# Decay rows of a four-batch attention kernel: one fp32 sum in place of a high and a low part, no zero rows, stacks made at first use, second job prepared before the first scores

## The chip, the cores and the metric

One core of a Trainium2 chip runs the whole program. The metric is device time in microseconds (us) of one execution, input and output in the chip's memory; a profile of one execution shows what each engine did. The engines are PE (TensorE: matmuls, with PEld its weight loads), DVE (VectorE), ACT (ScalarE), POOL (GpSimd) and SP, which here only issues DMAs, in the order of its program.

## The reference, cut to what matters

Decayed causal attention (4 batches, 8 heads, 576 positions, head size 64) feeds two feed-forward layers (512 to 2048 to 512) over 2304 tokens:

```
scores = (1/sqrt(64)) * q @ k^T
cum    = cumsum(log(clip(f, 1e-4, 1)))           # one number per position
scores = where(causal, scores + cum[i] - cum[j], -1e9)
attn   = softmax(scores);  y = attn @ v
x = y as (2304, 512)
h = x @ w_in;  x = (h * tanh(softplus(h))) @ w_out
h = x @ w2_in; out = (h * cos(h)) @ w2_out
```

## The kernel before

Attention runs as 20 jobs. A job is one pair of heads of one batch; batch 0 is cut into jobs 0 to 3 (query blocks 0 and 1) and jobs 4 to 7 (blocks 2 to 4), batches 1 to 3 have one job for each pair with all five blocks. An item is one block of one job. For an item PE makes the scores (L503 for batch 0, L510 later), DVE adds the mask and takes the row maximum (L553), ACT takes the exponential and its sum (L559), DVE inverts the sum (L570, L571), POOL scales (L573), PE transposes the probabilities three items later (L610, L599), and PE multiplies them by v (L635), from where ACT and DVE write the result `xb` (L647, L648). Once batch 0's first tokens are there, the first layer's matmuls with w_in (L154) are woven between attention items. After attention, only the feed-forward layers are left.

The decay enters the scores as extra rows of the contraction. A stack holds transposed q and transposed k in partitions 0 to 63 (L473 on ACT, L475 on DVE, from PE's transposes L450). In batch 0 (`whole(jb)`, fp32 stacks `stk0`, `stk1`) the rows 64, 65, 96 and 97 hold the decay sum as a high and a low part and the constants -1 and 1 that meet them; the other rows from 64 to 127 are set to zero, and the contraction is 128 rows long. Later jobs use fp32r stacks of four planes (`stkr0`, `stkr1`) in two passes; the second pass carries the decay the same way. Every stack is filled once by four memsets (L656 to L659), each over 32 partitions and 1152 elements.

The decay sum is made by `decay_tables`: a load of f, a clip, Ln, a scan (L751), then the high part on ACT (L753) and the low part on DVE (L754). Job 0's rows are copied from there to the stack by four DMAs (L426); both parts go to a DRAM buffer `cumd` (L434), and every later job's rows come from there (L428). `prep_job(jb)` issues these row copies, then the transposes and casts of q and k, then the loads of job jb+2. The weights of w_in are loaded in pieces of 512 KB (L105, no earlier than the copy to `cumd`) and converted by DVE, POOL and ACT (L124, L125, L129, L134, L138, L139). A scheduler sets the final order of each engine from dependencies and its own costs, so the order on an engine is not the order of the lines.

Of the kernel before, what the change touches and what calls it, by code (L numbers as in the profile page):

```python
# [32 lines left out]
def f(ap):  # L33
    return ap.bitcast(F32)
# [3 lines left out]
def tile_attention_two_ffn(  # L38
# [40 lines left out]
    yd = dram.tile([128, 2, NK, NT], F32, name="yd")  # L79
    cumd = dram.tile([B * H, 2, S], F32, name="cumd")  # L80
# [274 lines left out]
    def attention_units(p, bank):  # L355
# [11 lines left out]
        def whole(jb):  # L367
            return jobs[jb][0] // NP in CUT_BATCHES
# [47 lines left out]
        def prep_job(jb):  # L416
# [6 lines left out]
            for row, x in ((96, 0), (64, 1)) if whole(jb) else ((96, 2), (64, 3)):  # L423
                if jb == 0:
                    for y in range(2):
                        nc.sync.dma_start(out=st[row + y : row + y + 1, x], in_=cums[y][h0 : h0 + 2])  # L426
                else:
                    nc.sync.dma_start(  # L428
                        out=st[row : row + 2, x] if whole(jb) else f(st[row : row + 2, x]),
                        in_=cumd[h0 : h0 + 2].rearrange("h y s -> y h s")  # L430
                    )
            if jb == 0:
                for y in range(2):
                    marks["cum"] = nc.sync.dma_start(out=cumd[:, y], in_=cums[y])  # L434
# [12 lines left out]
            for g in groups:  # L447
# [3 lines left out]
                for which, lo in ((0, qlo), (1, 0)):  # L451
# [14 lines left out]
                    if whole(jb):  # L466
                        for j in range(2):
                            i_ = t[64 * j : 64 * j + 64, at : at + n * P]
                            if jb == 0:
                                i_ = i_.rearrange("r (c p) -> r c p", p=P)  # L470
                            o = part(slice(0, 64), which, j)
                            if which or j:
                                nc.scalar.activation(out=o, in_=i_, func=AF.Copy, scale=sc)  # L473
                            else:
                                nc.vector.tensor_scalar(out=o, in0=i_, scalar1=sc, scalar2=None, op0=ALU.mult)  # L475
                        continue
# [15 lines left out]
        def scores(jb, i):  # L492
# [7 lines left out]
            def product(o, j, c0, c1, first=QS[i], m=r):  # L500
                if whole(jb):
                    at = j * S + first
                    marks["score"] = nc.tensor.matmul(  # L503
                        o, lhsT=st.rearrange("p x j s -> p (x j s)")[0:128, at : at + m],
                        rhs=st[0:128, 1, j, c0:c1], start=True, stop=True,
                    )
                    return
                for x in range(2):
                    at = (4 * x + j) * S + first
                    marks["score"] = nc.tensor.matmul(  # L510
                        o, lhsT=st.rearrange("p x j s -> p (x j s)")[0:128, at : at + m],
                        rhs=st[0:128, 2 * x + 1, j, c0:c1], start=(x == 0), stop=(x == 1),
                    )
# [138 lines left out]
        def new_stack(pool, name, dt, en):  # L652
# [3 lines left out]
            nc.gpsimd.memset(q[96:128], 0.0)  # L656
            nc.gpsimd.memset(k[64:96], 0.0)
            en.memset(q[64:96], -1.0)
            en.memset(k[96:128], 1.0)  # L659
# [19 lines left out]
        stack(late - 1)  # L679
# [4 lines left out]
        for _ in prep_job(0):  # L684
            pass
        prep = None
# [7 lines left out]
        for m in range(2 * (M + LT + 1)):  # L694
# [14 lines left out]
            if m2 < M:  # L709
# [4 lines left out]
                if at == begin:  # L714
                    prep = prep_job(jb + 1)
# [28 lines left out]
    def decay_tables(p):  # L744
# [7 lines left out]
        ch, cl = (x.bitcast(F32R) for x in (ft, one))  # L752
        nc.scalar.activation(out=ch, in_=cum, func=AF.Copy)  # L753
        nc.vector.tensor_tensor(out=cl, in0=cum, in1=ft, op=ALU.subtract)  # L754
        cums.extend((ft, one))
# [140 lines left out]
```

## Time and profile before

| | |
|---|---|
| median of 3 runs | 1055.91 us (1055.45 to 1059.02) |
| the profiled execution | 1053.56 us, span of the trace 1051.8 us |
| PE | busy 1011.2 us, 96% of the span |
| DVE, ACT, POOL | 57%, 51%, 23% |
| DMA | 111.80 MB, mean 106 GB/s |

The profiled execution is itself 2.35 us below the median of the runs. PE is the engine to watch: 40.6 us of the span are not PE, and the question for each of them is which wait ended last.

### The profile page before, as it was taken

What the parts mean: (1) busy time and instruction counts of PE and PEld (TensorE: products, weight loads), DVE (VectorE), ACT (ScalarE), POOL (GpSimd) and SP (SyncE); (2) the same over time, 40 slices, a digit from 0 to 9 for tenths busy, and PEclk for the clock granted to TensorE, in tenths of its full rate; (3) what the DMA queues carried; (4) which work ended last, traced back from release to release, by engine and by line L of the source; (5) the groups of instructions that cost most, each with busy time, mean ns of one, the idle gap of its engine ahead of it and who ended that gap; (6) DMA issues with size and microseconds to landing.
All of it is one profiled execution on the core that took longest, in us unless ns stands there. A gap on an engine that the chain in (4) does not pass through costs nothing.

```text
span 1051.8 us, 16908 instructions
## 1 busy us (share of the span) xinstructions
PE 1011.2 (96%) x5920; PEld 865.8 (82%) x5920; DVE 598.3 (57%) x1402; ACT 537.6 (51%) x1142; POOL 236.9 (23%) x331
## 2 busy tenths in 40 slices
PE   5798899999999999999999999999999999999998
PEld 4586779899999999977778888888888888888897
DVE  5858755666555536746664267766444544454454
ACT  4666746665556536446664465644433333333343
POOL 7647643433323312412120012111000000000000
PEclk9999999999999999999999999999999999999999
DMA  4655423333331138756966365412100300110010
GB/s 118 169 151 123 136 70 95 85 93 89 84 90 60 57 117 277 238 176 196 325 206 223 111 195 177 159 41 71 50 1 1 120 1 1 41 41 1 1 41 21
DMA packets 118361, 111.80 MB, mean 106 GB/s; under 512 B 66564, under 2 KB 87044, under 8 KB 118276
## 3 DMA queue, kind: packets, MB, share of 16 engines
q1 hardware_dynamic: 118276, 110.72, 34.5%
q8 instruction: 47, 0.77, 0.3%
q14 instruction: 38, 0.31, 0.1%
HBM read 77.49 MB, written 33.18 MB: 105 GB/s over the span
## 4 chain that ended last, share of the span: by engine, by line
PE 77%; DMA 8%; DVE 5%; ACT 4%; issue 3%; POOL 3%; SPq 0%; ACTq 0%; POOLq 0%; DVEq 0%
PE h L154 24%; PE acc L257 19%; PE hx L154 9%; DMA hl<-hd 5%; PE s L635 5%; PE acc L249 5%; PE s L610 4%; PE s L510 3%; PE hx L249 2%; PE h L249 2%; PE s L450 2%; PE s L503 2%; DMA raw<-in_moe_w_in_dram 1%; POOL wol L139 1%; DVE gl L319 1%
## 5 line engine op out<-in xcount | busy, mean ns | idle before, releaser
L154 PE MATMUL h<-xb,wih 128*128 128x288 f32 (+2 forms) x848 | 184.2, 305 | 4.0 <-ACT wih L138 2.7
L154 PEld LDWEIGHTS h<-xb,wih 128*128 128x128 f32 x848 | 138.7, 191 | 7.1 <-ACT wih L138 3.2
L154 PE MATMUL h<-xb,wil 128*128 128x288 f32 (+2 forms) x424 | 126.3, 300 | 0.0
L559 ACT ACTIVATE s<-s,mx 128x448 f32<-128x448 f32 (+5 forms) x144 | 83.7, 582 | 68.4 <-DVE mx L553 64.4
L257 PE MATMUL acc<-woh,gh 128*128 128x512 f32 x288 | 112.9, 392 | 0.0
L257 PE MATMUL acc<-woh,gl 128*128 128x512 f32 x288 | 112.3, 391 | 0.0
L257 PE MATMUL acc<-wol,gh 128*128 128x512 f32 x288 | 112.0, 389 | 0.0
L573 POOL TENSOR_SCALAR s<-s,sm 128x448 f32<-128x448 f32 (+5 forms) x144 | 82.8, 588 | 124.4 <-DVE sm L571 63.4
L319 DVE TENSOR_TENSOR gl<-hl,gh 128x512 fp32r<-128x512 f32 x72 | 65.0, 904 | 70.5 <-ACT gh L314 70.4
L154 PE MATMUL hx<-x,wih 128*128 128x512 f32 (+1 forms) x320 | 92.7, 369 | 0.0
L154 PE MATMUL h<-x,wih 128*128 128x512 f32 (+1 forms) x320 | 91.0, 369 | 0.0
L305 ACT ACTIVATE n<-n 128x512 f32<-128x512 f32 (+1 forms) x80 | 47.1, 589 | 85.8 <-DVE n L299 85.6
L139 POOL TENSOR_TENSOR wol<-raw,woh 128x512 fp32r<-128x512 f32 x32 | 45.3, 1416 | 197.6 <-ACT woh L138 174.0
L553 DVE CUSTOM_DVE_ANT_0 s<-s,maskt 128x288 f32<-128x288 f32 (+6 forms) x152 | 63.7, 430 | 45.3 <-PE s L510 24.9
L319 DVE TENSOR_TENSOR gl<-e,gh 128x512 fp32r<-128x512 f32 (+1 forms) x80 | 53.8, 672 | 50.7 <-ACT gh L314 50.5
L154 PEld LDWEIGHTS h<-xb,wil 128*128 128x128 f32 x424 | 79.9, 190 | 1.3 <-issue 0.8
L298 DVE TENSOR_SCALAR n<-e 128x512 f32<-128x512 f32 (+1 forms) x80 | 32.7, 408 | 84.3 <-ACT e L291 83.8
L288 ACT ACTIVATE hl<-hl 128x512 f32<-128x512 f32 x72 | 45.1, 629 | 61.1 <-DMA hl<-hd 59.4
L314 ACT ACTIVATE gh<-e 128x512 fp32r<-128x512 f32 (+1 forms) x80 | 47.1, 588 | 52.3 <-DVE e L310 48.9
L249 PE MATMUL acc<-gl,woh 128*128 128x512 f32 (+1 forms) x192 | 68.5, 358 | 3.3 <-DVE gl L319 3.2
L249 PE MATMUL acc<-gh,wol 128*128 128x512 f32 (+1 forms) x192 | 67.8, 354 | 0.0
L154 PEld LDWEIGHTS h<-x,wih 128*128 128x128 f32 x320 | 58.4, 188 | 11.0
(119 smaller groups left out, 2215.7 us busy)
## 6 DMA issues: line engine op xcount, KB each, us to landing
hl<-hd SPq DMA_DIRECT2D x72, 256.0 KB
raw<-in_moe_w_in_dram SPq DMA_DIRECT2D x32, 512.0 KB
raw<-in_moe_w_out_dram SPq DMA_DIRECT2D x32, 512.0 KB
hd<-hs SPq DMA_DIRECT2D x48, 288.0 KB
yd<-stage SPq DMA_DIRECT2D x32, 256.0 KB
x<-yd SPq DMA_DIRECT2D x32, 256.0 KB
natk<-in_k_dram SPq DMA_DIRECT2D x32, 144.0 KB
out_dram<-stage SPq DMA_DIRECT2D x18, 256.0 KB
```

Of the source, the lines that this page charges most:

```text
L139: nc.gpsimd.tensor_tensor(out=lo[sl], in0=f(high), in1=f(hi[sl]), op=ALU.subtract)
L154: nc.tensor.matmul(o, lhsT=a[wsl], rhs=b[:, kk, :], start=(kk == 0 and i == 0), stop=(kk == NK - 1 and i == 2),)
L249: nc.tensor.matmul(acc[ti][d][:, 0:T], lhsT=a[dsl], rhs=b[:, gs], start=(start and i == 0), stop=(end and i == 2),)
L257: nc.tensor.matmul(acc[ti][m], lhsT=a[:, ms], rhs=b[:, j % 2, :], start=(start and i == 0), stop=(end and i == 2),)
L288: nc.scalar.activation(out=e, in_=e, func=AF.Mish, scale=UNSCALE)
L305: nc.scalar.activation(out=t, in_=t, func=AF.Sin, scale=TWO_PI)
L314: nc.scalar.activation(out=gh, in_=e, func=AF.Copy)
L319: marks["v1"] = nc.vector.tensor_tensor(out=gl, in0=st.pop(n)[0], in1=f(gst[n][0]), op=ALU.subtract)
L553: marks["ttr"] = nc.vector.tensor_tensor_reduce(out=s[rows, c0:c1], in0=o, in1=mk, scale=-1.0, scalar=BIG if prev is None or rows.start el ...
L559: nc.scalar.activation(out=s[:, 0:w], in_=s[:, 0:w], func=AF.Exp, scale=-1.0, bias=mx, accum_out=sm[:, j : j + 1])
L573: nc.gpsimd.tensor_scalar(out=s[:, 0:w], in0=s[:, 0:w], scalar1=sm[:, j : j + 1], scalar2=1.0, op0=ALU.mult, op1=ALU.mult)
L635: pair = nc.tensor.matmul(t[64 * j : 64 * j + 64, c0:width], lhsT=vt[jb][:, c, j], rhs=pt[:, j, c, c0:width], start=(c == 0), stop=(c == n ...
```

## The change

The decay sum stays one fp32 number. In batch 0 it is one row: row 65 of q's half and row 64 of k's half, with -1 and 1 opposite, and the contraction is 66 rows long. In later jobs the parts stay split, in rows 64 to 67, and the second pass is 68 rows long. The zero rows and their memsets go: two memsets for a stack, over 2 or 4 partitions. Job 0's and job 1's rows come straight from the scan's result in SBUF, those of jobs 2 to 7 from a new DRAM buffer `cumf`, those of later jobs from `cumd`. The split into high and low part (`decay_parts`) and the two copies to `cumd` are placed behind the first two steps of `prep_job(1)`, which now stand ahead of the first scores. The fp32r stack is made where it is first asked for. In job 0, both halves of q are cast by DVE.

```diff
-            for row, x in ((96, 0), (64, 1)) if whole(jb) else ((96, 2), (64, 3)):
-                if jb == 0:
-                    for y in range(2):
-                        nc.sync.dma_start(out=st[row + y : row + y + 1, x], in_=cums[y][h0 : h0 + 2])
-                else:
+            if whole(jb):
+                for row, x in ((64, 1), (65, 0)):
                     nc.sync.dma_start(
-                        out=st[row : row + 2, x] if whole(jb) else f(st[row : row + 2, x]),
-                        in_=cumd[h0 : h0 + 2].rearrange("h y s -> y h s")
+                        out=st[row : row + 1, x], in_=cums[0][h0 : h0 + 2] if jb < 2 else cumf[h0 : h0 + 2]
+                    )
+            else:
+                for row, x in ((64, 3), (66, 2)):
+                    nc.sync.dma_start(
+                        out=f(st[row : row + 2, x]), in_=cumd[h0 : h0 + 2].rearrange("h y s -> y h s")
                     )
             if jb == 0:
-                for y in range(2):
-                    marks["cum"] = nc.sync.dma_start(out=cumd[:, y], in_=cums[y])
+                marks["cum"] = nc.sync.dma_start(out=cumf, in_=cums[0])
...
-                            if which or j:
+                            if which or j and jb:
...
-                        o, lhsT=st.rearrange("p x j s -> p (x j s)")[0:128, at : at + m],
-                        rhs=st[0:128, 1, j, c0:c1], start=True, stop=True,
+                        o, lhsT=st.rearrange("p x j s -> p (x j s)")[0:66, at : at + m],
+                        rhs=st[0:66, 1, j, c0:c1], start=True, stop=True,
...
-                for x in range(2):
+                for x, rows in ((0, 128), (1, 68)):
...
-            nc.gpsimd.memset(q[96:128], 0.0)
-            nc.gpsimd.memset(k[64:96], 0.0)
-            en.memset(q[64:96], -1.0)
-            en.memset(k[96:128], 1.0)
+            rows = slice(64, 66 if one else 68)
+            en.memset(q[rows], -1.0)
+            en.memset(k[rows], 1.0)
...
-        stack(late - 1)
...
+        ahead = prep_job(1)
+        for _ in range(2):
+            next(ahead)
+        decay_parts()
...
-                    prep = prep_job(jb + 1)
+                    prep = prep_job(jb + 1) if jb else ahead
...
+    def decay_parts():
+        cum, hi, lo = cums
+        nc.scalar.activation(out=hi.bitcast(F32R), in_=cum, func=AF.Copy)
+        nc.vector.tensor_tensor(out=lo.bitcast(F32R), in0=cum, in1=hi, op=ALU.subtract)
+        for y, t in enumerate((hi, lo)):
+            nc.sync.dma_start(out=cumd[:, y], in_=t)
```

Three places show how this moves instructions. The line numbers of the changed kernel are one to seven higher than before (L105 is L106, L553 is L554, L648 is L649).

SP's queue from the first row copies on, before (`stk_107` is job 0's stack, `stk_123` job 1's, `natq` and `natk` the loads of a later job, `raw` two pieces of w_in):

```order
L426 DMA stk_107<-s 1x2x576 x4
L434 DMA cumd<-s 32x576 x2
L388 DMA natq<-in_q_dram 64x4x64 x2
L388 DMA natk<-in_k_dram 64x4x64 x2
L428 DMA stk_123<-cumd 2x2x576 x2
L105 DMA raw<-in_moe_w_in_dram 128x2x512 x2
L388 DMA natq<-in_q_dram 64x4x64 x2
L388 DMA natk<-in_k_dram 64x4x64 x2
L428 DMA stk_107<-cumd 2x2x576 x2
```

The same stretch in the changed kernel (`stk_106` and `stk_120` are the two stacks):

```order
L426 DMA stk_106<-s 1x2x576 x2
L435 DMA cumf<-s 32x576
L389 DMA natq<-in_q_dram 64x4x64 x2
L389 DMA natk<-in_k_dram 64x4x64 x2
L426 DMA stk_120<-s 1x2x576 x2
L762 DMA cumd<-s 32x576 x2
L389 DMA natq<-in_q_dram 64x4x64 x2
L389 DMA natk<-in_k_dram 64x4x64 x2
L106 DMA raw<-in_moe_w_in_dram 128x2x512 x2
L426 DMA stk_106<-cumf 1x1152 x2
```

Three DMAs are gone ahead of job 2's loads; the copies to `cumd` and job 3's loads now stand ahead of the two weight pieces, and job 2's row copies, which stood behind job 3's loads, stand directly behind the weights.

POOL at the start, before (`stkr_128` is the first fp32r stack, `maskt` and `mask_68` the causal masks, whose triangles the last two rows cut):

```order
L656 MEMSET stk_123 32x1152
L657 MEMSET stk_123 32x1152
L658 MEMSET stk_123 32x1152
L659 MEMSET stk_123 32x1152
L656 MEMSET stkr_128 32x1152
L657 MEMSET stkr_128 32x1152
L658 MEMSET stkr_128 32x1152
L659 MEMSET stkr_128 32x1152
L733 AFFINE_SELECT maskt<-maskt 128x128
L739 AFFINE_SELECT mask_68<-mask_68 64x64 x2
```

And in the changed kernel:

```order
L740 MEMSET mask_68 128x320
L658 MEMSET stk_120 2x1152
L659 MEMSET stk_120 2x1152
L658 MEMSET stkr_1068 4x1152
L659 MEMSET stkr_1068 4x1152
L736 AFFINE_SELECT maskt<-maskt 128x128
L742 AFFINE_SELECT mask_68<-mask_68 64x64 x2
```

Four memsets are gone ahead of the masks here, and two more of `stk0` further up; the scheduler has put the memsets of the fp32r stack at the same early place although the stack is now asked for only by job 8.

DVE where job 5's first block is masked, which is the last attention work ahead of the first L154 matmuls, before (`mask_68` marks that block, `xb<-s_629` is the write of `xb` that the next PSUM tiles wait for):

```order
L553 ISA s,mx<-s_621,mask_68 128x320
L553 ISA mx 128x1
L134 SCALAR_TENSOR_TENSOR raw<-raw 128x512
L570 TENSOR_SCALAR sm<-sm 128x2
L124 TENSOR_SCALAR raw<-raw 128x512
L571 RECIPROCAL sm<-sm 128x2
L570 TENSOR_SCALAR sm<-sm 128x1
L125 SCALAR_TENSOR_TENSOR raw<-raw 128x512
L571 RECIPROCAL sm<-sm 128x1
L648 TENSOR_TENSOR xb<-s_629,xb 128x256
```

And in the changed kernel:

```order
L125 TENSOR_SCALAR raw<-raw 128x512
L126 SCALAR_TENSOR_TENSOR raw<-raw 128x512
L571 TENSOR_SCALAR sm<-sm 128x2
L572 RECIPROCAL sm<-sm 128x2
L554 ISA s,mx<-s_612,mask_68 128x320
L554 ISA mx 128x1
L135 SCALAR_TENSOR_TENSOR raw<-raw 128x512
L571 TENSOR_SCALAR sm<-sm 128x1
L572 RECIPROCAL sm<-sm 128x1
L649 TENSOR_TENSOR xb<-s_620,xb 128x256
```

The two steps on the newest weight piece (L124, L125 before) have moved ahead of the mask of job 5's block; the same set of instructions still stands ahead of the write of `xb`.

## Rows read from the trace of the kernel before

**Rows 1.** The page: span, and PE's busy time, share and instructions.

```profile
span 1051.8 us, 16908 instructions
PE 1011.2 (96%) x5920; PEld 865.8 (82%) x5920; DVE 598.3 (57%) x1402; ACT 537.6 (51%) x1142; POOL 236.9 (23%) x331
```

**Rows 2.** Windows: length, busy PE, PEld, DVE, ACT, POOL, PE clock, DMA share, GB/s.

```profile
0.00:11.56 11.56, 1.35 (x8) 1.03 (x9) 5.63 (x6) 4.50 (x6) 10.60 (x19) 1.00 0.35 82
...
45.00:50.00 5.00, 0.85 (x9) 0.49 (x8) 4.01 (x16) 3.11 (x8) 2.50 (x6) 0.87 1.09 231
50.00:56.00 6.00, 6.00 (x21) 4.58 (x22) 2.96 (x4) 1.38 (x3) 4.80 (x5) 0.54 0.35 101
...
150.00:400.00 250.00, 249.41 (x1984) 230.22 (x1983) 136.87 (x505) 141.43 (x381) 75.11 (x144) 1.00 0.31 88
...
20.00:21.00 1.00, 1.00 (x4) 0.46 (x2) 0.26 (x1) 0.41 (x2) 0.42 (x1) 1.00 1.05 152
```

**Rows 3.** PE's waits in the first 60 us: total, times, longest.

```profile
PE s L503 <- DMA stk<-s: 5.7, 1, 5.7
...
PE s L599 <- DVE xb L648: 4.2, 1, 4.2
```

**Rows 4.** Timeline of SP's DMA issues from 7 to 20 us: start, duration.

```profile
7.58 2.73 SPq L426 DMA_DIRECT2D stk<-s  x4
10.37 0.86 SPq L434 DMA_DIRECT2D cumd<-s  x2
11.32 1.40 SPq L388 DMA_DIRECT2D natq<-in_q_dram  x2
12.81 1.25 SPq L388 DMA_DIRECT2D natk<-in_k_dram  x2
14.24 0.68 SPq L428 DMA_DIRECT2D stk<-cumd  x2
14.96 0.91 SPq L105 DMA_DIRECT2D raw<-in_moe_w_in_dram  x2
...
18.69 0.72 SPq L428 DMA_DIRECT2D stk<-cumd  x2
```

**Rows 5.** Timeline of the engines from 7 to 23 us.

```profile
7.29 1.90 ACT L473 ACTIVATE stk<-s 64x256 f32<-64x256 f32 x3
...
11.56 1.20 PE L503 MATMUL s<-stk 128*128 128x128 f32 x4 [5.67 <-DMA stk<-s]
...
13.76 0.29 POOL L733 TENSOR_SCALAR_AFFINE_SELECT maskt<-maskt 128x128 f32<-128x128 f32 x1
...
14.18 0.27 DVE L553 CUSTOM_DVE_ANT_0 s<-s,maskt 128x128 f32<-128x128 f32 x1
...
15.38 0.39 ACT L559 ACTIVATE s<-s,mx 128x128 f32<-128x128 f32 x1
...
16.46 1.20 PE L503 MATMUL s<-stk 128*128 128x128 f32 x4 [0.66 <-DMA stk<-cumd]
...
22.69 1.19 PE L503 MATMUL s<-stk 128*128 128x128 f32 x4 [1.56 <-DVE raw L125]
```

**Rows 6.** Timeline around the last stack's memsets, 94 to 104 us.

```profile
94.73 0.43 DVE L124 TENSOR_SCALAR raw<-raw 128x512 int32<-128x512 int32 x1 [1.16 <-DMA raw<-in_moe_w_in_dram]
...
98.30 1.05 POOL L659 MEMSET stkr<- 32x1152 f32 x1
...
98.51 1.13 DVE L124 TENSOR_SCALAR raw<-raw 128x512 int32<-128x512 int32 x1
...
99.44 0.71 POOL L129 TENSOR_SCALAR raw<-raw 128x512 f32<-128x512 f32 x1
...
103.94 0.91 PE L635 MATMUL s<-p,natv 128*64 128x64 f32 x12 [2.58 <-DVE p L594]
```

**Rows 7.** Weight loads by form from 56 to 150 us: busy, mean ns.

```profile
L610 PEld LDWEIGHTS s<-ident,s 128*128 128x128 f32 x110 | 13.0, 147 | 1.9 <-DVE stkr L481 1.5
...
L450 PEld LDWEIGHTS s<-ident,natk 96*128 96x128 f32 x30 | 3.6, 153 | 0.0
```

More of the change, by code (lines that the diff above doesn't have):

```diff
@@ L79, in tile_attention_two_ffn @@
     yd = dram.tile([128, 2, NK, NT], F32, name="yd")
+    cumf = dram.tile([B * H, S], F32, name="cumf")
     cumd = dram.tile([B * H, 2, S], F32, name="cumd")
@@ L503, in product @@
                     marks["score"] = nc.tensor.matmul(
-                        o, lhsT=st.rearrange("p x j s -> p (x j s)")[0:128, at : at + m],
-                        rhs=st[0:128, 1, j, c0:c1], start=True, stop=True,
+                        o, lhsT=st.rearrange("p x j s -> p (x j s)")[0:66, at : at + m],
+                        rhs=st[0:66, 1, j, c0:c1], start=True, stop=True,
                     )
                     return
-                for x in range(2):
+                for x, rows in ((0, 128), (1, 68)):
                     at = (4 * x + j) * S + first
                     marks["score"] = nc.tensor.matmul(
-                        o, lhsT=st.rearrange("p x j s -> p (x j s)")[0:128, at : at + m],
-                        rhs=st[0:128, 2 * x + 1, j, c0:c1], start=(x == 0), stop=(x == 1),
+                        o, lhsT=st.rearrange("p x j s -> p (x j s)")[0:rows, at : at + m],
+                        rhs=st[0:rows, 2 * x + 1, j, c0:c1], start=(x == 0), stop=(x == 1),
                     )
@@ L751, in decay_tables @@
         nc.vector.tensor_tensor_scan(out=cum, data0=one, data1=ft, initial=0.0, op0=ALU.mult, op1=ALU.add)
[L752 to L755, printed above, removed]
+        cums.extend((cum, ft, one))
+    def decay_parts():
[4 more added lines that the diff above has]
+            nc.sync.dma_start(out=cumd[:, y], in_=t)
     hidden = [(0, 256), (256, S - 256)] + [(b * S + x, S // 2) for b in range(1, B) for x in (0, S // 2)]
```

## The prediction

> **What bounds the kernel now.** I read the page first: PE is busy 1011.2 of a span of 1051.8 us [rows 1], so 40.6 us are not PE, and a change that neither shortens a matmul nor closes one of those gaps is worth nothing. Then the windows, to see where the gaps lie: between 150 and 400 us PE is busy 249.41 of 250.00 us, but it does 1.35 us of work in the first 11.56 us and 0.85 us between 45 and 50 [rows 2]. All that this change touches lies in the first part, and whatever start is won there is kept only if nothing else sets the pace before PE fills up. Then PE's waits: the two large ones are 5.7 us for job 0's row copies and 4.2 us for a write of `xb` [rows 3]. The second has a tail: in the 6.00 us behind it the granted clock is 0.54, most of it at 1.2 GHz instead of 2.4, after PE had stood nearly idle for 5 us [rows 2]. Last I read SP's queue and the engines' timeline through the first three jobs, since those show what PE waits for there [rows 4, 5].
>
> **Shorter contraction: 0.** Score matmuls go from 128 rows to 66 in batch 0 and, in the second pass, to 68 later. Their columns stay. The nearest rows on the effect of contraction length are two groups of weight loads of 128 columns: 96 rows take 153 ns on average, 128 rows 147 ns [rows 7]. Fewer rows are not faster, so I price all score matmuls as unchanged. The low end would be a gain in proportion to rows; nothing in these two groups points there.
>
> **First scores: 1.37 us earlier.** PE's first score matmul starts at 11.56 us, ended by the row copies. SP issues four of them from 7.58 in 2.73 us, 0.68 each, and PE starts 11.56 - 10.31 = 1.25 us behind the last issue [rows 4, 5]. Two issues remain, so PE may start at 11.56 - 2 x 0.68 = 10.19. SP was not free earlier, so that the sum need not be split first gains nothing in SP's start at 7.58. The casts of job 0 do not replace the wait: ACT's three take 0.63 each from 7.29 [rows 5], and two remain for job 0, over by 8.6. The second rival to the copies, the mask, goes away too: its triangle is cut at 13.76 behind a row of memsets, and the first masking runs at 14.18, the first exponential at 15.38 [rows 5]. Six memsets less at 1.05 each [rows 6] put the triangle near 7.5. With scores over at 10.19 + 1.20 = 11.39, masking starts 2.8 us earlier than before. This is the larger head start, but it is one of DVE and ACT, not of PE.
>
> **Second job's scores: 1.10 us earlier.** They start at 16.46, ended by copies that SP had issued by 14.24 + 0.68 = 14.92 [rows 4, 5]. New queue: 7.58 + 1.37 (two copies) + 0.43 (one store) + 1.40 + 1.25 (loads) + 1.37 (two copies) + 0.42, the gaps between these groups in [rows 4], is 13.82. With the same 1.54 us to PE: 15.36. PE so waits longer here than before, since its own work arrives earlier.
>
> **Third job's scores: this is where most of it goes.** They need row copies that now stand behind the two weight pieces. SP reaches those after 13.82 + 0.86 (stores) + 2.65 (loads, as the pair above) and about 0.3 of gaps, at 17.6 instead of 14.96: 2.6 us later. The copies behind them are issued at 18.6 to 19.3 instead of 18.69 to 19.41 [rows 4]. Before, PE started 22.69 - 19.41 = 3.28 us behind the issue, against 1.54 for the second job; in between the DMA share was 1.05 [rows 2, 5]. (The trace puts this wait down to a weight instruction of DVE, which PE's score matmul does not read; I take it for the copies.) If only the issue mattered, the third job would start at 19.3 + 1.54 = 20.8, 1.9 us earlier. If the bytes ahead of the copies matter, they are the same 1 MB of weights and the same loads, and they start to be issued at about the same time (14.7 against 14.96), so the gain is about 0.1. The nearest row is this very wait, which lies by the second reading. Against it stands that DVE, ACT and POOL have done more of jobs 0 and 1 by then, and give some back later. I take 1.0 us, between 0 and 1.9.
>
> The Trainium skill ("DMA: Bandwidth & Descriptors", section "Queues, rings and completion order") says that a DMA's completion signal lands only after every earlier write of the same DMA engine, so that a small copy behind large transfers is reported as late as they are. By that rule the copies cannot be done before the weights, and the term would be 0.1; by the row of the second job alone it would be 1.9.
>
> **The hole at 45 to 50 us: 0.** PE waits 4.2 us there for a write of `xb` [rows 3]. On DVE the two weight steps move ahead of one block's mask, but the same instructions stand ahead of the write, so I price it at 0. On ACT, one more weight cast (0.63 by the nearest cast [rows 5]) comes ahead of its half of `xb`: up to 0.6 later. The other end is that the hole closes: 4.2.
>
> **The last stack's memsets: 0.7 us.** In the old kernel four POOL memsets run into the conversion of a weight piece: L124 takes 1.13 us beside the memset that ends at 99.35, and 0.43 elsewhere [rows 6]. POOL's next step follows directly at 99.44, and 4.5 us later PE ends a wait of 2.58 us for DVE. Two memsets go, 2.1 us of POOL. DVE is the engine PE waits for, so I take DVE's own loss, 1.13 - 0.43 = 0.70; the ends are 0 and 2.1.
>
> **Extra work at no cost.** The store to `cumf` and both stores to `cumd` lie on SP ahead of loads that are needed a job later, and are counted above. The split of the sum (ACT, DVE) now runs beside the first transposes; job 8 is the first to read it, tens of us later. If that cover went, it would cost some 1.3 us once, as two casts of 0.63 [rows 5].
>
> **Sum.** 1.0 + 0 + 0.7 = 1.7 us. The profiled execution goes from 1053.56 to 1051.9, and since it lies 2.35 below the median, the median goes from 1055.91 to 1054.2.
>
> **The rivals.**
> The head start is kept and the hole shrinks. For it: the mask comes 2.8 us earlier and the hole waits for DVE and ACT, not for PE. Against it: the third job's copies. With 1.9 for the copies, 2.1 for POOL, half of the 4.2 us hole, and 1.0 of the 2.8 us (6.00 x 0.46) that the low clock behind it costs, the gain is 7.1: 1048.8.
>
> The change does nothing. The new order on SP only moves the wait from the first job to the third, POOL's memsets were covered, and the matmuls keep their length: 1055.9.
>
> It becomes slower, through the weight pieces that SP issues 2.6 us later. For it: the changed DVE takes the newest piece ahead of a block's mask, so a late piece now holds back attention as well, and ACT casts a piece ahead of `xb`. Against it: the first w_in matmul only comes around 50 us. It decides if a piece lands later than DVE has finished the four masks ahead of it; each us behind that point goes straight into the hole. With the whole 2.6 us, ACT's 0.6 and 1.0 for a longer stretch at the low clock, less 0.7 from POOL: 3.5 us slower, 1059.4. A second such stretch, 2.8 us, would bring 1062.
>
> **How the numbers follow.** About 0.5%, 5.3 us, is what a measurement of this kernel tells from no change. The forecast (1052 to 1056) has 0.44, the kept head start 0.27, no effect 0.14, slower 0.15. Of the kept head start 0.22 lies beyond 5.3 us, of the slower case 0.08 does: faster 0.22, same 0.70, slower 0.08. The range leaves out a tenth on either side: down to 1046.5, where hole and low clock both go for the most part, and up to 1058.5, most of the slow rival's price.
>
> **What would show it.** The first score matmul near 10.2 us, the first exponential near 12, the second job's scores near 15.4 with a longer wait than 0.66, the third job's between 20.8 and 22.7: that row decides between forecast and rival. The score matmuls keep their mean durations by form. In the window from 45 to 56 PE's wait for `xb` and the low clock are still there. Around 95 us two memsets of 1.05 instead of four, and no L124 of 1.13. The prediction is wrong if the hole closes, if w_in's pieces appear among PE's waits ahead of 60 us, or if the time between 150 us and the end changes by more than 1 us.

## The result and the profile after

The changed kernel takes 1064.14 us (median of 6 runs, 1062.44 to 1069.01), the kernel before 1055.78 in the same comparison (1054.16 to 1059.02): ratio 1.0082, 95% interval 1.0064 to 1.0101. It is 8.4 us slower; the forecast was 1.7 us faster. The profiled execution is one of 1063.74 us. TensorE has more busy time with the same number of instructions, where [rows 1] has 1011.2 us:

```profile
span 1062.0 us, 16920 instructions
PE 1022.5 (96%) x5920; PEld 870.5 (82%) x5920; DVE 597.5 (56%) x1403; ACT 538.2 (51%) x1141; POOL 226.4 (21%) x323
```

The windows of the changed kernel, columns as in [rows 2]. Behind 150 us PE is as full as before; from 38 to 62 us the clock stands at 0.50, which is 1.2 GHz, where the kernel before has only 48.7 to 55.6 so (0.87 and 0.54 in its windows of [rows 2]):

```profile
31.00:38.00 7.00, 3.54 (x29) 2.60 (x27) 4.05 (x15) 3.77 (x13) 1.66 (x4) 1.00 0.70 181
38.00:45.00 7.00, 6.12 (x16) 2.75 (x18) 5.15 (x19) 4.38 (x12) 5.76 (x8) 0.50 0.60 142
45.00:50.00 5.00, 5.00 (x23) 3.95 (x20) 3.49 (x10) 3.75 (x9) 2.52 (x4) 0.50 0.47 136
50.00:56.00 6.00, 5.41 (x20) 2.63 (x18) 4.50 (x15) 3.50 (x8) 3.89 (x5) 0.50 0.62 161
56.00:62.00 6.00, 4.96 (x18) 4.17 (x19) 0.98 (x2) 0.82 (x3) 2.07 (x4) 0.50 0.50 137
...
150.00:400.00 250.00, 249.00 (x1977) 229.24 (x1977) 139.56 (x522) 142.34 (x387) 78.06 (x150) 1.00 0.30 84
```

PE's waits in the first 60 us of the changed kernel, which answer to [rows 3]. The wait for `xb` is small now; those for the third job's row copies and for a cast of ACT are new or larger:

```profile
PE s L504 <- ACT stk L474: 4.3, 1, 4.3
...
PE s L504 <- DMA stk<-cumf: 3.5, 1, 3.5
PE s L504 <- DMA stk<-s: 2.3, 1, 2.3
PE s L504 <- DVE sm L571: 1.8, 1, 1.8
PE s L600 <- DVE xb L649: 1.5, 1, 1.5
```

Rows picked out of SP's issues and of the engines' timeline in the changed kernel, as in [rows 4, 5]: first scores, first mask and exponential, second and third job's scores, and then the hole that ends at 38.88:

```profile
7.56 1.41 SPq L426 DMA_DIRECT2D stk<-s  x2
...
17.40 1.11 SPq L106 DMA_DIRECT2D raw<-in_moe_w_in_dram  x2
18.61 0.56 SPq L426 DMA_DIRECT2D stk<-cumf  x2
```

```profile
10.21 2.90 PE L504 MATMUL s<-stk 66*128 66x128 f32 x8 [2.33 <-DMA stk<-s]
11.55 0.29 DVE L554 CUSTOM_DVE_ANT_0 s<-s,maskt 128x128 f32<-128x128 f32 x1 [3.10 <-PE s L504]
11.89 0.40 ACT L560 ACTIVATE s<-s,mx 128x128 f32<-128x128 f32 x1 [2.11 <-DVE mx L554]
14.90 1.20 PE L504 MATMUL s<-stk 66*128 66x128 f32 x4 [1.79 <-DVE sm L571]
23.11 0.43 DVE L125 TENSOR_SCALAR raw<-raw 128x512 int32<-128x512 int32 x1 [0.35 <-DMA raw<-in_moe_w_in_dram]
23.11 1.19 PE L504 MATMUL s<-stk 66*128 66x128 f32 x4 [3.55 <-DMA stk<-cumf]
26.14 2.07 PE L504 MATMUL s<-stk 66*128 66x256 f32 x4
36.23 0.43 DVE L125 TENSOR_SCALAR raw<-raw 128x512 int32<-128x512 int32 x1 [1.90 <-DMA raw<-in_moe_w_in_dram]
36.58 0.69 DVE L135 SCALAR_TENSOR_TENSOR raw<-raw 128x512 int32<-128x512 int32 x1
37.30 0.67 ACT L139 ACTIVATE wih<-raw 128x512 fp32r<-128x512 f32 x1 [1.06 <-DVE raw L135]
37.87 0.97 ACT L474 ACTIVATE stk<-s 64x384 f32<-64x384 f32 x2
38.88 1.34 PE L504 MATMUL s<-stk 66*64 66x320 f32 x4 [4.35 <-ACT stk L474]
41.06 3.19 PE L504 MATMUL s<-stk 66*128 66x448 f32 x4
57.04 0.87 PE L600 MATMUL s<-ident,s 128*128 128x128 f32 x3 [1.46 <-DVE xb L649]
```

Read upwards from 38.88: PE waits for a cast of keys, that stands on ACT behind a weight cast, which waits for a step on one weight piece, and that stands on DVE behind the first step on the next piece, which waits for its load. The first w_in matmul comes at 57.56 us instead of 50.39, 7.2 us later. The two profiled executions lie 10.2 us apart, so most of their difference arises ahead of that point; a second trace of each kernel (e11 and e12, below) has 2.8 us there. The last stack's memsets, two now, as in [rows 6]:

```profile
101.43 1.05 POOL L658 MEMSET stkr<- 4x1152 f32 x1
102.08 0.69 DVE L125 TENSOR_SCALAR raw<-raw 128x512 int32<-128x512 int32 x1 [1.98 <-DMA raw<-in_moe_w_in_dram]
102.42 1.34 POOL L659 MEMSET stkr<- 4x1152 f32 x1
```

### The profile page after: what moved, and what is told of

It reads as the page before. It is cut to its first block, busy times and chain, and to the rows that moved or that the text cites. A ratio compares the mean times of both kernels' runs of the same rounds, so it can differ in the third digit from the quotient of the medians.

```text
span 1062.0 us, 16920 instructions
## 1 busy us (share of the span) xinstructions
PE 1022.5 (96%) x5920; PEld 870.5 (82%) x5920; DVE 597.5 (56%) x1403; ACT 538.2 (51%) x1141; POOL 226.4 (21%) x323
## 5 line engine op out<-in xcount | busy, mean ns | idle before, releaser
L554 DVE CUSTOM_DVE_ANT_0 s<-s,maskt 128x288 f32<-128x288 f32 (+6 forms) x152 | 63.8, 432 | 43.3 <-PE s L511 17.3
L289 ACT ACTIVATE hl<-hl 128x512 f32<-128x512 f32 x72 | 45.1, 629 | 61.9 <-DMA hl<-hd 57.6
L636 PE MATMUL s<-p,natv 128*64 128x256 f32 (+3 forms) x544 | 62.0, 371 | 7.1 <-DVE p L595 5.2
```

Of the source, the lines that this page charges most:

```text
L289: nc.scalar.activation(out=e, in_=e, func=AF.Mish, scale=UNSCALE)
L554: marks["ttr"] = nc.vector.tensor_tensor_reduce(out=s[rows, c0:c1], in0=o, in1=mk, scale=-1.0, scalar=BIG if prev is None or rows.start el ...
L636: pair = nc.tensor.matmul(t[64 * j : 64 * j + 64, c0:width], lhsT=vt[jb][:, c, j], rhs=pt[:, j, c, c0:width], start=(c == 0), stop=(c == n ...
```

## The experiments

A run's time stands with its ratio to the kernel before, which was measured beside it, and the 95% interval of the ratio. A hole is a stretch in which PE waits, a filler is work for PE whose result nobody reads. The first w_in matmul is used as a milestone: from there on PE has the first layer's matmuls to fill its time.

**First theory: the hole at 34.5 to 38.88 us, and the low clock behind it, make the loss.** Rivals: the low clock alone, the place of the second job, the row layout.

*e1.* One order held on DVE, so that the weight step no longer stands behind the next piece.

```diff
+                if early and i == 3:
+                    hold.enter_context(tc.issue_after(marks["conv"].ins))
...
-                nc.vector.scalar_tensor_tensor(
+                marks["conv"] = nc.vector.scalar_tensor_tensor(
                     out=high, in0=high, scalar=3, ...
```

> The changed kernel, with one order held on VectorE: the last step on the third weight piece (L135 of the changed kernel) comes ahead of the first step on the fourth (L125), which in the changed kernel stands ahead of it and waits 1.90 us for its piece until 36.23. Theory (the hole at 34.5 to 38.88 us and the low clock behind it make most of the 8.4 us): L135 then runs near 34.4 instead of 36.58, ACT's weight cast and the two 64x384 casts of the stack follow about 2 us earlier, PE's wait falls from 4.35 us to about 2.4, near the 2.36 of the kernel before, which kept the clock; the clock stays at 1.00 up to 45 us, the first w_in matmul comes at 50 to 53 us instead of 57.56, and the time is about 1057 (2 for the hole and about 5 for the clock less than 1064.1). Rival A (late weight pieces alone): the wait only moves, the first w_in matmul stays near 57 us, 1062 to 1064. Rival B (the row layout or the shorter contraction costs time all along): 1062 at best, with the gain of the hole alone.

1063.85 us, ratio 1.0091 (1.0073 to 1.0108). The wait did fall, from 4.35 to 0.65 us, and nothing was won in the total: the first w_in matmul comes at 55.7, and the same four matmul instructions of 448 columns (two fp32 matmuls) still take 3.19 us at 40.19. So the hole's length by itself does not make the loss. Whether closing it would have held a high clock, this run cannot say: here the clock rose only at 46.9 us, so that it was low with the hole closed as well.

*e2.* 24 transposes of the identity that nobody reads, put in the hole.

```diff
... (last: the key transposes of this group)
+                if jb == 4 and g is groups[-1]:
+                    w = bank()
+                    with tc.issue_after(last.ins):
+                        for _ in range(24):
+                            nc.tensor.transpose(w[:, 0:128], ident, ident)
```

> The changed kernel with 24 transposes of the identity that nobody reads, put on PE behind the last key transposes of job 4, so that PE works in most of the hole at 34.5 to 38.88 us; nothing that the scores wait for is to come earlier, so the scores stay at about 38.9. Theory (the clock, not the hole's own length, costs most): PE is busy until about 37.7, the clock stays at 1.00 in 38 to 45 us, the first w_in matmul comes near 52 us, the time is about 1059. Rival A (VectorE and ScalarE set the pace up to 57 us, and the low clock is hidden behind them): clock back at 1.00, but the first w_in matmul stays within 1 us of 57.5 and the time at 1064. Rival B (the filler delays the transposes behind it): later than 58 us, 1065 or more.

1060.44 us, ratio 1.0054 (1.0039 to 1.0068): 4.8 us above the kernel before, where the changed kernel lies 8.4 above it, with nothing taken away. The clock rose at 37.3 us, 0.9 us behind the filler's start at 36.46, and stayed up to 51.0; the first w_in matmul came at 54.0. So the clock does set a part of the time.

*e3 and e4.* e3 is without the head start of the second job. e4 is e3 with the fp32r stack made at the start and job 0's casts divided as in the kernel before; of the change it keeps the row layout with its memsets, the row copies from the unsplit sum and the later place of the split.

```diff
-        ahead = prep_job(1)
-        for _ in range(2):
-            next(ahead)
         decay_parts()
...
-                    prep = prep_job(jb + 1) if jb else ahead
+                    prep = prep_job(jb + 1)
```

> The changed kernel without the head start of the second job: its row copies and transposes stand where the kernel before has them, and the split of the decay sum directly behind the first job's preparation. Rows, stacks, memsets and copies stay as changed. SP then issues the first two weight pieces ahead of the fourth job's loads, as before. Theory (the loss comes from the place of the weight pieces in the order, not from the rows): no PE wait over 3 us between 30 and 45 us, clock 1.00 there, 1054 to 1058. Rival (rows, contraction or the late-made stack): 1062 to 1065.

> The row layout alone: as the run without the head start, and also the fp32r stack made at the start and the casts of the first job divided between VectorE and ScalarE as in the kernel before. So against the kernel before only the unsplit rows, the contraction of 66 and 68 rows, the two short memsets in place of four and the place of the split differ. Theory: first scores about 1.4 us earlier than 11.56, nothing else of size, 1053 to 1057. Rival (rows or contraction cost): 1060 to 1065, with longer score matmuls by form.

1062.18 (1.0063, 1.0044 to 1.0082) and 1061.83 us (1.0065, 1.0041 to 1.0088). The row layout as e4 has it brings most of the loss, with no PE wait over 1.6 us between 20 and 60 us. Windows of e4 (PE alone, then clock, DMA share, GB/s) beside two of its timeline rows:

```profile
38.00:45.00 7.00, 5.88 (x16) 1.00 0.64 178
45.00:50.00 5.00, 5.00 (x25) 1.00 0.26 58
```

```profile
41.30 3.19 PE L504 MATMUL s<-stk 66*128 66x448 f32 x4
47.88 4.10 PE L504 MATMUL s<-stk 66*128 66x288 f32 x8
```

The clock column says 1.00 and the matmuls run at half pace: 3.19 us where four of 448 columns take 1.67 at the full level, 2.4 GHz. The column shows 1.00 up to the first change of level in the record (e4: 60.3 us), so ahead of it the durations count, in every kernel here.

**Second theory (B): the contraction of 66 and 68 rows keeps the clock down.** The rival (C) is the order of the work, since in most of these runs the scheduler wrote another one when the rows changed.

*e5, e6, e10.* e5 is the kernel before with 68 rows, e6 the changed kernel with zero rows up to 127 again, e10 the layout of e4 with these zero rows.

```diff
-            for row, x in ((96, 0), (64, 1)) if whole(jb) else ((96, 2), (64, 3)):
+            for row, x in ((66, 0), (64, 1)) if whole(jb) else ((66, 2), (64, 3)):
... (e6 and e10)
+            nc.gpsimd.memset(q[64:128], 0.0)
+            nc.gpsimd.memset(k[64:128], 0.0)
...
-                        o, lhsT=st.rearrange("p x j s -> p (x j s)")[0:66, at : at + m],
-                        rhs=st[0:66, 1, j, c0:c1], start=True, stop=True,
+                        o, lhsT=st.rearrange("p x j s -> p (x j s)")[0:128, at : at + m],
+                        rhs=st[0:128, 1, j, c0:c1], start=True, stop=True,
```

> The kernel before, with the decay rows moved next to each other (rows 64 to 67) and the score matmuls shortened to 68 rows of contraction, 128 before; memsets (the same number and size), copies, high and low part and the second job's place stay. The scheduler then writes a somewhat other order. Reason for it: in the four runs so far PE's clock first rose at 37 to 60 us where the kernel before has 31.7, and what they share is the contraction of 66 rows. Theory B (the short contraction delays the rise of the clock): matmuls are at half pace until 40 us or later, the first w_in matmul comes at 54 to 58 us instead of 50.4, the time is 1059 to 1064. Theory C (the places of the holes in PE's work, that is the order alone, decide on the clock): the rise stays near 31 us and the time at 1054 to 1058.

> The changed kernel with zero rows again up to row 127 (two memsets of 64 partitions more for a stack) and a contraction of 128 rows in both passes; unsplit sums, copies, first use and the second job's head start stay as changed. Theory B: PE's clock rises at 32 us or earlier and stays up to 45 us at least, the first w_in matmul comes by 53 us, the time is 1055 to 1059. Theory C: the rise may come at 31 us as in the changed kernel's own trace, but the hole at 34.5 us and the low clock behind it stay, 1061 to 1065.

> The row layout alone, as in the run that has it with a contraction of 66 rows and took 1061.8 us, but with zero rows and 128 rows of contraction. Theory B: the clock rises at 32 us or earlier instead of 60, the first w_in matmul comes at 50 to 53 us instead of 56.9, 1054 to 1058. Theory C: the order of that run decides, with its waits near 33 and 37 us; the rise comes after 45 us and the time stays at 1059 to 1063.

1061.06 (1.0051, 1.0037 to 1.0066), 1058.46 (1.0022, 1.0009 to 1.0035) and 1059.36 us (1.0043, 1.0027 to 1.0059). Fewer rows cost the kernel before 5.6 us. Each taken against the kernel before beside it, zero rows give the changed kernel 5.4 us back, and e4 2.1; this last one is not clear of the noise, since the intervals of e4 and e10 overlap, and e10's time lies where C had it. The clock first rose at 46.5 us in e5 (31.7 in the kernel before, whose order on PE is the same up to 30.5 us), at 13.8 in e6 and at 20.6 in e10 (60.3 in e4). In e6 the two rows that were shown of e4 read:

```profile
37.15 1.67 PE L504 MATMUL s<-stk 128*128 128x448 f32 x4
40.60 2.13 PE L504 MATMUL s<-stk 128*128 128x288 f32 x8
```

*e11, e12.* One more trace of each kernel, for the clock.

> The kernel before once more, for one look at its clock: is the rise at 31.7 us and the fall at 48.7 us the same in another execution? If the contraction of 128 rows carries it, the rise comes by 32 us again. If the rise is a matter of chance, it comes at 37 to 60 us in a good share of looks.

> The changed kernel once more, for one look: its first trace had the rise at 31.2 us and a fall at 38.1 us. If the place of its holes fixes this, both come at the same places. If the short contraction leaves the rise to chance, it comes at 46 us or later, as in four of the runs with 66 to 68 rows, and the first w_in matmul at 54 us or later either way.

The rise alone does not part them (28.6 and 31.8 us), and it was not left to chance in the changed kernel: rise and fall came where its first trace has them (31.8 and 38.7 us, 31.2 and 38.0 there). The time at the full level ahead of the first w_in matmul does part them: 17.0 and 17.1 us before, 6.8 and 6.9 after. In the kernel before it came in one piece the first time (31.7 to 48.7) and in two the second (28.6 to 35.4 and from 42.2), so that the equal sums are partly luck.

*e13.* The contraction by itself: nine blocks of 60 fp32 matmuls behind the last work of the changed kernel.

```diff
+    for rows in (128, 66, 128, 66, 128, 66, 128, 96, 98):
+        for _ in range(24):
+            nc.gpsimd.memset(x, 0.5)
+        w = hbank()
+        for _ in range(60):
+            nc.tensor.matmul(w[:, 0:256], lhsT=x[0:rows, 0:128], rhs=x[0:rows, 256:512], ...)
```

> The contraction by itself. The changed kernel, and behind its last work nine blocks of 60 fp32 matmuls of 256 columns on one constant tile, back to back, each block behind a pause in which GpSimd fills the tile 24 times; rows of contraction by block: 128, 66, 128, 66, 128, 66, 128, 96, 98. Its time as a whole is of no interest. Theory B in its plain form (fewer rows keep the clock from rising): the blocks of 128 rows go from half to full pace within some 10 us and take about 20 us, those of 66 rows stay at half pace much longer and take 25 to 32 us. Rival (rows do not matter to the clock; it was the mixture of work around the scores): all blocks take the same time, within 3 us.

```profile
1056.56 26.06 PE L881 MATMUL hx<-probe 128*128 128x256 f32 x120
1096.70 51.57 PE L881 MATMUL h<-probe 66*128 66x256 f32 x120 [14.08 <-POOL probe L878]
1162.35 29.12 PE L881 MATMUL hx<-probe 128*128 128x256 f32 x120 [14.08 <-POOL probe L878]
1205.55 51.57 PE L881 MATMUL h<-probe 66*128 66x256 f32 x120 [14.08 <-POOL probe L878]
1271.20 27.62 PE L881 MATMUL hx<-probe 128*128 128x256 f32 x120 [14.08 <-POOL probe L878]
1312.90 51.57 PE L881 MATMUL h<-probe 66*128 66x256 f32 x120 [14.08 <-POOL probe L878]
1378.55 28.55 PE L881 MATMUL hx<-probe 128*128 128x256 f32 x120 [14.08 <-POOL probe L878]
1421.18 29.41 PE L881 MATMUL h<-probe 96*128 96x256 f32 x120 [14.08 <-POOL probe L878]
1464.67 28.16 PE L881 MATMUL hx<-probe 98*128 98x256 f32 x120 [14.08 <-POOL probe L878]
```

That settles, for fp32 matmuls of 66 rows, that they do not raise the clock: with the same columns and the same pause ahead, blocks of 66 rows run to their end at half pace, 51.57 us each, while the blocks of 96, 98 and 128 rows take 27.62 to 29.41 us, since the clock rises inside them. (The first block, 26.06 us, follows the kernel's work without a pause and finds the clock up.) It does not say whether 66 rows let a raised clock fall, nor where between 66 and 96 rows the change lies. The Trainium skill ("TensorE: Matmul & The Clock Gate", Part 1: The HAM clock gate) says that the clock follows how busy the engine has been; here TensorE was busy without a gap for 51.57 us and stayed at 1.2 GHz, so here the measurement differs from the page, and it decides.

*e14, e15.* Fillers as matmuls of 66 or of 128 rows in three holes (the code is that of e7, below).

> The changed kernel with matmuls as fillers in the same three places and numbers as in the run of the changed kernel with fillers (1052.2 us), but each with 66 rows of contraction. Up to the first fillers nothing differs. Theory B: the first 14 fillers at 19.4 us do not raise the clock, which rises after 30 us; the first w_in matmul comes at 54 us or later; 1057 to 1062. Rival: the clock rises near 22.5 us as with 128 rows, 1051 to 1054.

> The same with 128 rows of contraction in each filler, as the counterpart (matmuls in place of transposes, else as the run of 1052.2 us). Theory B: the clock rises near 22.5 us, 1051 to 1054. Rival: no difference beyond 1.5 us between this run and its counterpart of 66 rows.

e14 takes 1.0107 (1.0061 to 1.0153) and e15 1.0053 (1.0035 to 1.0071) times what the kernel before takes. Up to the first filler both kernels are the same. With 66 rows the clock first rose at 58.9 us, with 128 at 20.9:

```profile
19.37 6.18 PE L381 MATMUL s<-ident 66*128 66x128 f32 x28
```

```profile
19.34 4.04 PE L381 MATMUL s<-ident 128*128 128x128 f32 x28
```

The clock came as B has it, the times did not: e14's 1057 to 1062 and e15's 1051 to 1054 were misses. A filler matmul is two instructions here (x28 for 14), so these fillers last longer than the transposes of e7: the second and third take 10.50 and 5.63 us in e14, 6.11 and 5.62 in e15, and the work behind them starts without a wait, so that they held it up.

*e16, e18.* The changed kernel with 96 rows. Its order on PE is that of the changed kernel up to the first w_in matmul, on DVE and ACT up to 42 and 47 us, but for the memsets and masks of the start. Then the same kernel once more.

```diff
... (0:96 in place of 0:66 and 0:68 in the score matmuls)
+            nc.gpsimd.memset(k[64:96], 0.0)
-            en.memset(q[rows], -1.0)
+            en.memset(q[64:96], -1.0)
```

> The changed kernel with a contraction of 96 rows instead of 66 and 68: rows up to 95 are zero on one side (one memset more for a stack). The scheduler's order on TensorE is the same for the first 100 instructions, on ScalarE for the first 48, on VectorE for the first 75 but for the memsets, so that up to the first w_in matmul rows alone differ. Theory B: TensorE's clock is at its full level for 12 us or more ahead of the first w_in matmul (6.8 us in both looks at the changed kernel), that matmul comes 2 to 5 us earlier than 57.6 and 56.3, the time is 1057 to 1060. Theory C (order): 57 us again and 1062 to 1065.

> The kernel with 96 rows once more, for one look. In its first look the first w_in matmul came at 53.2 us, 3 to 4 us earlier than in the changed kernel, but the part from there to the last product with v took 351.9 us, where the other looks have 338 to 348, and that execution was the slowest of six. If this loss belongs to the kernel, the second look shows 349 us or more again; if it is chance, 342 to 346 and a time of 1059 to 1062. The first w_in matmul should come at 51 to 54 us in either case if the rows carry the clock.

The time at the full level came as B has it, 17.0 and 13.6 us. The first w_in matmul came at 53.2 and 56.1 us (57.6 and 56.3 in the changed kernel), so the second trace missed the 51 to 54 expected of it.

The traces fall into two pairs that differ, up to 42 us, in the rows and these memsets alone. The first part of e13 is the changed kernel a third time, in unchanged order; it has a hole of 2.92 us where e16 has 2.89. In both the clock falls behind the hole, at 38.6 and 39.0 us. With 96 rows it is back at 42.4, with 66 only at 59.0. The two lower rows of each block below are the same matmuls, e13 first:

```profile
37.92 0.76 PE L504 MATMUL s<-stk 66*64 66x320 f32 x4 [2.92 <-ACT stk L474]
39.52 3.19 PE L504 MATMUL s<-stk 66*128 66x448 f32 x4
46.10 4.10 PE L504 MATMUL s<-stk 66*128 66x288 f32 x8
```

```profile
38.05 0.76 PE L504 MATMUL s<-stk 96*64 96x320 f32 x4 [2.89 <-ACT stk L474]
39.44 3.15 PE L504 MATMUL s<-stk 96*128 96x448 f32 x4
44.38 2.13 PE L504 MATMUL s<-stk 96*128 96x288 f32 x8
```

In the other pair the holes are 4.35 us (changed kernel) and 4.39 (e18), the falls at 38.0 and 37.8, the returns at 61.9 and 48.0. So the fall follows the hole with either number of rows, and the rows decide when the clock comes back. The first w_in matmul comes 2.9 and 1.5 us earlier with 96 rows.

The total did not follow: 1063.71 us, ratio 1.0081 (1.0055 to 1.0107). From the first w_in matmul to the last product with v it takes 351.9 and 349.6 us, where both other kernels take 342.5 to 344.1. Both traced executions took longer than this kernel's median (1069.8 and 1069.2 us against 1063.7), so a median run may lose less there. In e16 the clock falls four times between 100 and 160 us (100.4, 117.5, 131.2, 151.6), twice in the changed kernel, whose window stands first (columns as in [rows 2]):

```profile
100.00:160.00 60.00, 50.32 (x364) 42.44 (x364) 38.84 (x123) 33.46 (x86) 32.78 (x49) 0.91 0.45 123
100.00:160.00 60.00, 50.62 (x339) 39.78 (x337) 43.50 (x142) 36.43 (x97) 35.90 (x51) 0.80 0.33 85
```

The records there show 24.0 us at 1.2 GHz against 10.2. Half of the difference, 7 us, is an estimate of what that costs, near the 7.8 by which this part is longer.

**Holding the clock up by other means: e7, e8, e9, e17.** Fillers in three holes of the changed kernel; of the kernel before; of the changed kernel with 128 and with 96 rows.

```diff
+        def idle_work(after, n):
+            w = bank()
+            with tc.issue_after(after.ins):
+                for _ in range(n):
+                    nc.tensor.transpose(w[:, 0:128], ident, ident)
... (behind the first two transposes of probabilities, job 4's key transposes, job 3's products with v)
+                    idle_work(last, 14)
+                    idle_work(last, 24)
+                idle_work(pair, 24)
```

> The changed kernel with transposes of the identity that nobody reads in three holes of PE: 14 behind the first two transposes of probabilities (near 19.5 us), 24 behind job 4's key transposes (near 35 us), 24 ahead of the first w_in matmuls (near 50 us). The clock is so held up by other means than by the scores. If the low clock makes the loss: the first rise comes by 25 us, no fall ahead of 50 us, the first w_in matmul by 51 us and at full pace, and the time is 1054 to 1057, 2 us of it from the pace behind 50 us. If VectorE and ScalarE set the pace up to there: the rise comes as said, but the first w_in matmul stays at 53 to 54 us as with one filler, 1059 to 1060.

> The kernel before with the same kind of filler in the same three places, sized to its shorter waits (7, 14 and 28 transposes). It shows what the order of the kernel before is worth where the clock is held up in both. If the low clock is all that parts the two kernels, its time lies within 1.5 us of the changed kernel with fillers; if the order counts as well, it lies 3 us or more below. In any case the clock should not fall at 48.7 us, which gives back up to 2.8 us: 1052 to 1055.

> The changed kernel with the fillers in three holes, and with zero rows and a contraction of 128 rows as well. Theory B (the short contraction lets the clock fall even where PE has work): the clock that rises near 22.5 us with the first filler no longer falls at 39.8 us as in the run with fillers alone, no stretch at half pace between 25 and 60 us is longer than 7 us, the first w_in matmul comes 1 to 3 us earlier than 52.6, the time is 1049 to 1052. Theory C (order alone): the clock falls at 39 to 40 us again, 1052 to 1054, the memsets costing up to 1 us.

> The changed kernel with a contraction of 96 rows and with fillers in the three holes, 14, 16 and 12 transposes (14, 24 and 24 in the run of 1052.2 us, where work stood ready behind the third). Theory B: the clock stays up by the fillers and the rows together, the first w_in matmul comes at 50 to 51.5 us and at full pace, 1050 to 1052. Rival (VectorE and ScalarE set the pace there): as the run with 128 rows and fillers, 1053 to 1055.

1052.16 (0.9967, 0.9946 to 0.9989), 1054.30 (0.9988, 0.9974 to 1.0002), 1053.70 (0.9991, 0.9977 to 1.0006) and 1054.88 us (0.9987, 0.9972 to 1.0001). In e7 the clock rises at 22.7 us, as the first filler ends (31.2 without it), and the score matmuls behind it take 1.13 us where the changed kernel has 2.07:

```profile
19.36 3.19 PE L381 MATMUL s<-ident 128*128 128x128 f32 x14
...
24.96 1.13 PE L513 MATMUL s<-stk 66*128 66x256 f32 x4
```

So the changed kernel with fillers is the fastest run of all, 3.3 us below the kernel before beside it (1055.46). It also lies 2.1 below the kernel before with fillers (7, 14 and 28 transposes there), but the intervals of e7 and e8 overlap, and e8 itself is not clear of the kernel before. At least the order of the changed kernel shows no cost once the clock is held up. Rows and fillers do not add up in the total: e9 and e17 missed their forecasts of the time by 2 to 3 us. Their clocks came as B had it: in e7 (66 rows) the clock fell at 39.8 us, in e9 (128 rows) it stayed up from 30.5 to 98.8 and in e17 (96 rows) from 23.2 to 94.8. e17 has the first w_in matmul at 47.4 us, 5.2 earlier than e7, and lost it again behind: 344.6 us to the last product with v against 338.1.

## Why the prediction was wrong

All traces without fillers but e13's (full level: us at 2.4 GHz ahead of the first w_in matmul; middle: from there to the last product with v; median: of all runs of the kernel, in us):

| kernel | rows | full level | first w_in | middle | median |
|---|---|---|---|---|---|
| before, two traces | 128 | 17.0, 17.1 | 50.4, 53.5 | 343.3, 342.5 | 1055.8 |
| e5 | 68 | 6.6 | 53.1 | 343.4 | 1061.1 |
| changed, two traces | 66 | 6.8, 6.9 | 57.6, 56.3 | 344.1, 343.1 | 1064.1 |
| e1 | 66 | 6.8 | 55.7 | 347.6 | 1063.9 |
| e3, e4 | 66 | 0, 0 | 56.9, 56.9 | 342.6, 345.5 | 1062.2, 1061.8 |
| e6, e10 | 128 | 23.8, 20.4 | 51.1, 51.2 | 344.9, 344.5 | 1058.5, 1059.4 |
| e16, e18 | 96 | 17.0, 13.6 | 53.2, 56.1 | 351.9, 349.6 | 1063.7 |

The six traces with 66 or 68 rows have 0 to 6.9 us at the full level and the first w_in matmul at 56.1 us on average; the six with 96 or more have 13.6 to 23.8 and 52.6. (e13's first part, the changed kernel again, has 6.8, 56.0 and 343.1.)

- **Shorter contraction: 0.** The step that failed. The durations at a given clock came as priced: four matmul instructions of 128 columns take 1.20 us with 66 rows as with 128 [rows 5]. But a price by durations left out that the rows decide on the clock itself. Put at 0, the term measured 5.6 us (e5 against the kernel before) and 5.4 (the changed kernel against e6); two other pairs, below, show less. Nor is the clock column's 1.00 ahead of 31 us in [rows 2] the full level: the four instructions take 1.20 us at 11.56 us [rows 5], and 0.68 where e7 has 2.4 GHz (at 23.27).
- **First scores, second job's scores.** Right in size: 10.21 us (10.19 forecast), mask at 11.55 and exponential at 11.89, second job at 14.90 (15.36).
- **Third job's scores: 1.0 us earlier.** Wrong: 23.11, 0.4 later. They start 3.9 us behind the last copy's issue (19.17) with two weight pieces ahead, and at the same 23.11 DVE ends its wait for the second piece; the reading by bytes, not by issue, was the right one (the starts that the prediction names, 14.7 and 14.96, make its gain 0.26, not 0.1), and the head start ends there. The rule of the Trainium skill that the prediction cites ("DMA: Bandwidth & Descriptors", "Queues, rings and completion order"), on completion behind earlier writes, fits this row.
- **Hole at 45 to 50 us: 0.** It closed to 1.5 us, which the prediction names as a sign of being wrong. PE at half pace came later to it: with 96 rows, in the same order on PE and back at the full level earlier, the wait is 3.5 us in both traces. A new hole, 4.35 us, opened ten us earlier through late weight pieces, as the slow rival had it, in another place; shortening it to 0.65 in e1 won nothing in the total.
- **Last stack's memsets: 0.7 us.** No L124 of 1.13 any more (0.69, L125 in the changed kernel), two memsets instead of four, each as long over 4 partitions (1.05 and 1.34 us) as over 32 (1.05); a gain of this size can't be seen in the total.
- **The slow rival** had the sign and gave 1059.4. Its mechanism, late weight pieces, is not the main cause: e3, which has them ahead of job 3's loads again, still takes 1062.18 us. Its clock term (1.0, or 2.8 for a second stretch) was too small.

The two traces of each kernel lie 6.5 us apart on average, of which 5.0 arise ahead of the first w_in matmul (52.0 against 57.0). What the rows make of these lies between 2.3 (96 rows, same order on PE: 54.7) and 5.9 (128 rows in e6, with another order on DVE and ACT: 51.1). In the total, the four pairs that differ in rows show 5.6 us (e5), 5.4 (e6), 2.1 (e10, within the noise) and 0.4 (e16, whose traces lost the gain behind the first w_in matmul). How the rest of the 8.4 us divides, 3.0 and 4.1 us that e6 and e10 still lack, stays open: the scheduler writes another order with each change of rows, and e16 shows that clock falls at 100 to 160 us can be worth several us by themselves. Why the chip treats 66 rows so, no run shows.

## What to carry to other kernels

Rows of zeros in a contraction are not always free to remove (66 and 68 rows here, against 96 and more): price a shorter contraction by its durations and also by what it does to TensorE's clock where its busy stretches are broken by waits, as they are here in the first 60 us. Read the pace from durations of one form along the timeline, above all ahead of the first recorded change of the clock. Where a hole can't be closed, a few transposes of 128 rows that nobody reads, sized to the wait, may be worth more than a better order; fillers that outlast the wait give a part of it away again (e15 with 1060.55 us, e7 with 1052.16).

## What was not expected of the hardware

60 fp32 matmuls of 66 rows, back to back for 51.57 us, never left 1.2 GHz in three blocks of three; 96 rows took 29.41 us, with the rise inside the block.

What lets a raised clock fall is less clear. In e7 it fell at 39.8 us, though PE had waited for only 1.20 us of the 5 us ahead; its work there was score matmuls of 66 rows (0.76 and 1.67 us) and, with 128 rows, transposes of probabilities and products with v. In e9, with 128 rows in the scores, it stayed up through a wait of 2.51 us that ended at 41.83, and in e17, with 96, through one of 1.34 that ended at 43.27. That speaks for the rows. Against it stands e14: there the third filler, 24 matmuls of 66 rows, ran for 5.63 us from 63.38 at full pace, and the clock, up since 58.9, stayed so until 113.6. No run parts these.
